# Two ways for the conditional slots of a mixture-of-experts tail: a short one for up to 32 tokens and the full one

## The chip, the cores and the metric

One Trainium2 chip; the program runs on one core. The metric is the device time of one execution in microseconds, here the median of three runs.

## What is computed

An attention layer over 8 batches, 8 heads, 576 positions and 64 dimensions is compressed to 32 memory slots; its output, 4608 rows of 512, goes through a dense ELU network (512 to 2048 to 512), and that through a mixture of 8 experts where each token takes one expert:

```python
logits = x @ w_gate                      # 4608 x 8
expert_idx = np.argmax(logits, axis=1)
gate_w = softmax(logits)[token, expert_idx]
for e in range(8):
    mask = expert_idx == e
    h = np.maximum(x[mask] @ w1[e], 0.0) # 512 -> 1024
    out[mask] = gate_w[mask, None] * (h @ w2[e])
```

Everything is float32. With the inputs that are timed, the reference sends 576, 0, 1152, 576, 1703, 576, 0 and 25 tokens to experts 0 to 7. The first token's expert is 4.

## The kernel before, in words

The attention and the dense network fill the span until about 841 us. They write the rows of `x`, already times the gate, to the DRAM tensor `table`, and the tokens' numbers, sorted by expert, to `itab`. What follows is `phase2`, the expert stage.

Its unit is a **slot**: up to 288 tokens (T) of one expert. Expert 4's first two slots are computed early, while the dense network still runs or just after it (slots -2 and -1). `slots()` then counts on VectorE (DVE) how many slots each expert needs beyond those, and `control()` writes a table `ctl` with a row for each slot j: whether new expert weights must be loaded, and which expert. There are at least 14 more slots (NMIN = 14: numbers 0 to 13) and at most 23 (NS); `tot` says how many there are. For these inputs there are 15, so the slots that run are -2, -1 and 0 to 14. Slots 0 to 13 are written out in line; slots 14 to 22 stand in nested conditionals (`tc.If(end > j)`, L1255) on a register that all engines load from `ends` (L1250). Slot 14 is expert 3's second slot and holds its tokens 289 to 576.

A slot's work, per function:

- `gather(j)` (L715, issued by POOL): three indirect DMAs fetch the tokens' rows into `xr`. `x_store` and `x_load` (L729 and L733, issued by SyncE, SP) pass them through DRAM into `xg`; `x_turn` (L747, DVE) transposes them, and `x_split` (L752 ACT, L753 DVE) writes each value as a rounded part and a rest, `xh` and `xl`.
- `mm1(j, f)` (L1065): 12 TensorE (PE) matmuls into one of two PSUM buffers `ps_h`, then ReLU by ACT (L1068, `hh`) and its rest by DVE (L1069, `hl`), for f = 0 to 7. `mm2(j, f)` (L1080): 12 matmuls into four accumulators.
- `w1_split`, `w2_split` (L1047/1048 and L1053/1054): for the **next** slot, ACT copies 128x512 of the raw weights to the rounded part and DVE subtracts it for the rest; 16 pairs a slot. The conditional slots do them whether or not the next slot exists.
- `evac(j)` (L1088): four DVE transposes from the accumulators into `ot`. `o_store` (L738) writes `ot` to DRAM in four DMAs, all by SP, or two by SP and two by ACT (`TWO`, in the conditional slots). `o_load` (L741, SP) reads them back into `xr` by token, and `scatter` (L1093, POOL) sends them to `out` in three indirect DMAs; places without a token are dropped by the bounds check.
- `load(j, i)` (L1102, L1103, L941): SP loads two registers from `ctl` and issues a weight DMA that moves nothing where its condition is 0.

`columns()` (L1021 to L1029) turns the list of the tokens' numbers by three PE transposes into `idx` and `idw`, the columns from which gather and scatter take their places.

The order of all instructions is written out by hand; each engine takes its own in that order. SP and POOL are first-in, first-out: a DMA that waits holds up all behind it. In `slot(14)` of before, `gather(15)`, `x_store` and `x_load` come first, then the products with two weight splits behind each pair, `load(16, 0)`, `load(16, 1)`, and the store and scatter of slot 14, although slot 15 does not exist. Where a conditional is not taken, each engine instead runs a short block of accounting (rows with L1255 or L1260): it waits for its own work and DMAs that are under way, and raises the semaphores by what the skipped code would have. L1260 is the last conditional (`again`), which is not taken either.

## Time and profile before

| | |
|---|---|
| median of 3 runs | 1319.31 us (1316.88 to 1322.4) |
| profiled execution | 1317.07 us |
| its span, first to last instruction | 1315.4 us |
| busy PE | 1214.9 us (92%) |
| busy DVE | 817.2 us (62%) |
| busy ACT | 674.7 us (51%) |
| busy POOL | 471.4 us (36%) |
| mean granted TensorE clock | 0.973 |

Times in the rows are counted in us from the span's start. Busy shares are means over stages that differ; the stages that matter here are `phase2` from 841 us on, the last conditional slot (1264 to 1290 us), and the way of its result to `out` after that. L numbers are lines of the kernel before. A `q` behind an engine's name marks its sequencer, which branches, waits and issues DMAs.

### The profile page before, as it was taken

To read this page: it belongs to the slowest core of one execution; us is meant where nothing else is said; L and a number is where in the kernel's file an instruction comes from. 1 tells how busy PE (TensorE), PEld (TensorE's weight loads), DVE (VectorE), ACT (ScalarE), POOL (GpSimd) and SP (SyncE) were. 2 spreads that over 40 slices of the span, in tenths; PEclk is the share of its full clock that TensorE was granted. 3 is DMA by queue.
4 is the path that set the end of the run, shared out by engine and by line. 5 is a ranking of instruction groups with operands and counts; after the bars stand their busy time and mean duration, and the time that the engine had idled before them with its cause. 6 is when DMAs were issued, how large, how long until landed. Compare 5 with 4: busy or idle time off the path is not lost.

```text
span 1315.4 us, 26563 instructions
## 1 busy us (share of the span) xinstructions
PE 1214.9 (92%) x10137; PEld 1127.5 (86%) x10137; DVE 817.2 (62%) x1835; ACT 674.7 (51%) x1542; POOL 471.4 (36%) x502
## 2 busy tenths in 40 slices
PE   4497897999999999999999999999999999999992
PEld 2286776889899899898898999999999999999992
DVE  5899764655655656556556545744676767676763
ACT  3686544455555555565555556423444554454441
POOL 2556242443343444434434443411232123222020
PEclk9599998999999999999999999999999999999996
DMA  9776655543544436345432262125587887657633
GB/s 229 201 207 202 186 106 107 131 115 53 137 104 79 131 92 99 102 92 100 133 61 55 70 197 55 37 65 144 154 224 204 261 258 211 197 125 211 178 99 104
DMA packets 116795, 181.38 MB, mean 138 GB/s; under 512 B 11113, under 2 KB 82281, under 8 KB 113072
## 3 DMA queue, kind: packets, MB, share of 16 engines
q1 hardware_dynamic: 107680, 159.15, 47.4%
q0 software_dynamic: 8368, 20.11, 5.4%
q8 instruction: 83, 1.36, 0.5%
q14 instruction: 56, 0.46, 0.2%
q10 hardware_dynamic: 608, 0.30, 0.1%
HBM read 181.78 MB, written 44.47 MB: 172 GB/s over the span
## 4 chain that ended last, share of the span: by engine, by line
PE 71%; DMA 8%; DVE 6%; ACT 6%; issue 4%; POOL 3%; SPq 1%; DVEq 0%; POOLq 0%; ACTq 0%
PE ps_acc L551 23%; PE ps_h L1065 15%; PE ps_h L520 13%; PE ps_acc L1080 13%; PE ps_M L482 2%; DMA kv<-in_v_dram 2%; PE ps_kv L380 1%; DVE e L529 1%; DMA table<-yr 1%; PE ps_s L424 1%; DMA big<-in_q_dram 1%; ACT e L528 1%; DMA xd<-xr 1%; POOL sT L439 1%; ACT e L527 1%
## 5 line engine op out<-in xcount | busy, mean ns | idle before, releaser
L537 POOL TENSOR_TENSOR gl<-e,gh 128x288 fp32r<-128x288 f32 x237 | 195.9, 827 | 389.7 <-ACT gh L536 328.2
L520 PE MATMUL ps_h<-ath,wt 128*128 128x288 f32 x1024 | 261.7, 311 | 9.7 <-DVE e L529 8.4
L529 DVE SCALAR_TENSOR_TENSOR e<-e,ps_h 128x288 f32<-128x288 f32 x256 | 114.9, 449 | 214.5 <-ACT e L528 187.9
L520 PEld LDWEIGHTS ps_h<-ath,wt 128*128 128x128 f32 x1024 | 181.2, 191 | 54.1 <-issue 29.0
L536 ACT CAST gh<-e 128x288 fp32r<-128x288 f32 x256 | 110.3, 432 | 195.2 <-DVE e L529 193.4
L551 PE MATMUL ps_acc<-gh,wt 128*128 128x288 f32 x1024 | 178.3, 296 | 2.6 <-ACT gh L536 2.5
L551 PE MATMUL ps_acc<-gl,wt 128*128 128x288 f32 x1024 | 178.2, 296 | 1.7 <-DVE gl L537 1.7
L551 PE MATMUL ps_acc<-gh,wl 128*128 128x288 f32 x1024 | 178.4, 296 | 0.0
L1065 PE MATMUL ps_h<-xh,wt 128*128 128x288 f32 x1088 | 173.9, 299 | 3.1 <-ACT xh L752 1.6
L1068 ACT ACTIVATE hh<-ps_h 128x288 fp32r<-128x288 f32 x136 | 56.0, 412 | 232.2 <-PE ps_h L1065 214.8
L1065 PEld LDWEIGHTS ps_h<-xh,wt 128*128 128x128 f32 x1088 | 153.2, 188 | 9.6 <-ACT xh L752 5.7
L551 PEld LDWEIGHTS ps_acc<-gh,wt 128*128 128x128 f32 x1024 | 150.4, 189 | 3.8 <-ACT gh L536 3.7
L520 PE MATMUL ps_h<-atl,wt 128*128 128x288 f32 x512 | 152.8, 298 | 0.5 <-POOL atl L470 0.5
L551 PEld LDWEIGHTS ps_acc<-gl,wt 128*128 128x128 f32 x1024 | 150.5, 189 | 2.3 <-DVE gl L537 2.3
L551 PEld LDWEIGHTS ps_acc<-gh,wl 128*128 128x128 f32 x1024 | 151.4, 189 | 0.0
L1069 DVE SCALAR_TENSOR_TENSOR hl<-ps_h,hh 128x288 fp32r<-128x288 f32 x136 | 62.0, 456 | 131.8 <-ACT hh L1068 120.9
L1093 POOL DMA_INDIRECT out_dram<-xr,idw x45 | 47.0, 1043 | 251.0 <-DMA xr<-od 225.9
L527 ACT ACTIVATE e<-ps_h 128x288 f32<-128x288 f32 x256 | 104.6, 409 | 52.0 <-PE ps_h L520 41.8
L528 ACT ACTIVATE e<-e 128x288 f32<-128x288 f32 x256 | 113.8, 445 | 8.1
L520 PEld LDWEIGHTS ps_h<-atl,wt 128*128 128x128 f32 x512 | 98.0, 191 | 0.7 <-POOL atl L470 0.7
L1080 PE MATMUL ps_acc<-hh,wl 128*128 128x288 f32 x640 | 97.9, 294 | 0.0
L1065 PE MATMUL ps_h<-xl,wt 128*128 128x288 f32 x544 | 95.4, 297 | 1.3 <-DVE xl L753 1.3
(194 smaller groups left out, 1948.3 us busy)
## 6 DMA issues: line engine op xcount, KB each, us to landing
raw<-in_moe_w_dram SPq DMA_DIRECT2D x34, 2048.0 KB
win<-win_s SPq DMA_DIRECT2D x28, 1024.0 KB
xd<-xr SPq DMA_DIRECT2D x18, 576.0 KB
xg<-xd SPq DMA_DIRECT2D x72, 144.0 KB
xr<-od SPq DMA_DIRECT2D x17, 576.0 KB
od<-ot SPq DMA_DIRECT2D x66, 144.0 KB
kv<-in_k_dram SPq DMA_DIRECT2D x16, 576.0 KB
kv<-in_v_dram SPq DMA_DIRECT2D x16, 576.0 KB
```

What stands on the lines that cost most here:

```text
L520: nc.tensor.matmul(ps, x[:, u, fo:fo + P], y[:, u], start=(n == 0), stop=(n == 3 * NQ - 1))
L527: nc.scalar.activation(out=e, in_=ps, func=AF.Relu, scale=-1.0)
L528: nc.scalar.activation(out=e, in_=e, func=AF.Exp, scale=-1.0)
L529: nc.vector.scalar_tensor_tensor(out=e, in0=e, scalar=-1.0, in1=ps, op0=ALU.add, op1=ALU.max)
L536: nc.scalar.copy(out=gh, in_=e)
L537: eng.tensor_tensor(out=gl, in0=e, in1=gh.bitcast(F32), op=ALU.subtract)
L551: nc.tensor.matmul(acc[c], x[:, f, P * c:P * c + P], y, start=(first and n == 0), stop=(final and n == 2),)
L1065: nc.tensor.matmul(ps, w1_at(p, y, c, f), x[:, c], start=(n == 0), stop=(n == 3 * NC - 1))
L1068: nc.scalar.activation(out=h, in_=ps, func=AF.Relu)
L1069: V.scalar_tensor_tensor(out=l, in0=ps, scalar=0.0, in1=h.bitcast(F32), op0=ALU.max, op1=ALU.subtract)
L1080: nc.tensor.matmul(acc[c], w2t[p][:, y, f, P * c:P * c + P], x, start=(f + n == 0), stop=(f == NF2 - 1 and n == 2),)
L1093: d = nc.gpsimd.indirect_dma_start(out=out, out_offset=IndirectOffsetOnAxis(ap=at(n), axis=0), in_=xp["r"][:, n], in_offset=None, bounds_c ...
```

## The change

`slot` now does slots 0 to 13 alone, and it loads no weights and fetches no rows for a slot past the 14th. `control()` computes a third column of `ctl`: 2 where a slot holds at most 32 tokens (FEW), else 1; `columns()` makes a fourth transpose and a copy `idf`, the first 32 tokens' numbers. The registers `end`, `again` and this column of slot 14 (`first`) are loaded on all engines ahead of slot 13 and not behind it. A conditional slot then has two bodies under conditionals of their own. `many(j)` is the full slot: it first fetches slot j + 1 (loads, gather, store and load) under a conditional `end > j + 1`, does the products, and makes the 16 weight splits for the next slot in f = 3 to 6, four a step, ahead of `evac`; the transposes and splits of `x` for the next slot stand behind the scatter. `some(j)` multiplies 32 tokens' columns in plain float32, unsplit, straight from the raw weights, and writes them with one scatter.

```diff
--- before.py
+++ after.py
@@ -968,6 +968,7 @@
     V = nc.vector
     NMIN = NT // T - NE
     HN = NF2 // 2
+    FEW = 32
     ONE, TWO = [nc.sync], [nc.sync, nc.scalar]
     w2t = [wl.rearrange("p (y f) n -> p y f n", y=2), None]
 
@@ -981,7 +982,8 @@
     row, sb, rowi = tl(1, "row"), tl(E, "sb"), tl(1, "rowi", I32)
     its = const.tile([NS, T], I32, name="its")
     idx, idw = (const.tile([PR, NG * NS], I32, name=n) for n in ("idx", "idw"))
-    sj, ej, later, ctl, ends = tl(1, "sj"), tl(1, "ej"), tl(1, "later"), tl(2, "ctl", I32), tl(2, "ends", I32)
+    idf = const.tile([FEW, NS], I32, name="idf")
+    sj, ej, later, ctl, ends = tl(1, "sj"), tl(1, "ej"), tl(1, "later"), tl(3, "ctl", I32), tl(2, "ends", I32)
 
     def pick(o, w, x):
         V.tensor_tensor(out=tmp, in0=x, in1=w, op=ALU.mult)
@@ -1013,6 +1015,11 @@
         V.tensor_scalar(out=later, in0=pcol, scalar1=0.0, scalar2=None, op0=ALU.is_gt)
         V.scalar_tensor_tensor(out=ctl[:, 0:1], in0=sj, scalar=pcol, in1=later, op0=ALU.is_equal, op1=ALU.mult)
         V.tensor_copy(out=ctl[:, 1:2], in_=ej)
+        pick(sj, ind, ne)
+        V.tensor_tensor(out=row, in0=row, in1=jm, op=ALU.add)
+        V.scalar_tensor_tensor(out=row, in0=ej, scalar=-float(NR0), in1=row, op0=ALU.mult, op1=ALU.add)
+        V.scalar_tensor_tensor(out=sj, in0=row, scalar=-float(T), in1=sj, op0=ALU.mult, op1=ALU.add)
+        V.tensor_scalar(out=ctl[:, 2:3], in0=sj, scalar1=float(FEW), scalar2=1.0, op0=ALU.is_le, op1=ALU.add)
         V.tensor_copy(out=ends[:, 0:1], in_=tot)
         V.tensor_copy(out=ends[:, 1:2], in_=few)
 
@@ -1024,6 +1031,8 @@
             nc.tensor.transpose(
                 ps[0:PR, NS * n:NS * n + NS], itf.rearrange("j (p n) -> j n p", n=NG)[:, n], ident[0:NS, 0:NS],
             )
+        nc.tensor.transpose(ps[0:FEW, NS * NG:NS * NG + NS], itf[:, 0:FEW], ident[0:NS, 0:NS])
+        V.tensor_copy(out=idf, in_=ps[0:FEW, NS * NG:NS * NG + NS])
         ps = ps[0:PR, 0:NG * NS]
         V.tensor_scalar(out=idx, in0=ps, scalar1=float(NT - 1), scalar2=None, op0=ALU.min)
         V.tensor_copy(out=idw, in_=ps)
@@ -1095,33 +1104,35 @@
                 bounds_check=NT - 1, oob_is_err=False,
             )
             if not alone:
-                tc.declare_no_dep(d.ins, group="rows", reason="a token's row is its own")
-                tc.add_to_no_dep_group("rows", d.ins)
+                rows_out(d)
 
     def load(j, i):
         c, = (nc.values_load(ctl[j:j + 1, 0:1], engines=[SP], min_val=0, max_val=1),)
         ev = nc.values_load(ctl[j:j + 1, 1:2], engines=[SP], min_val=0, max_val=E - 1)
         load_raw(nc, raw[i], (w1, w2)[i], ev, c)
 
-    def slot(j, head, follow):
-        nxt = j + 1 < NS
-        p = (j + 1) % 2
-        if not head and j > 0:
+    def rows_out(d):
+        tc.declare_no_dep(d.ins, group="rows", reason="a token's row is its own")
+        tc.add_to_no_dep_group("rows", d.ins)
+
+    def splits(j, some):
+        for n in some:
+            w1_split(j % 2, n) if n < NF2 else w2_split(j % 2, n - NF2)
+
+    def x_splits(j, some=range(NC)):
+        for c in some:
+            x_split(j, c)
+
+    def slot(j):
+        follow = j + 1 < NMIN
+        if j > 0:
             o_store(ONE)
         if j < NMIN - 1:
             gather(j + 2)
         if 0 < j < NMIN - 1:
             x_store()
-        if not head and j > 0:
+        if j > 0:
             scatter(of(idw, j - 1))
-        if j >= NMIN and nxt:
-            gather(j + 1)
-            x_store()
-            x_load()
-        turn = 3 if j < NMIN else NF2 - 1
-        if head:
-            mm1(j, 0)
-            mm1(j, 1)
         for f in range(NF2):
             if f + 2 < NF2:
                 mm1(j, f + 2)
@@ -1131,30 +1142,84 @@
             if f == NF2 - 1:
                 evac(j)
                 if not follow:
-                    o_store(TWO if j >= NMIN else ONE)
+                    o_store(ONE)
                     scatter(of(idw, j))
-            if nxt:
-                for n in range(2):
-                    if f < HN:
-                        w1_split(p, 2 * f + n)
-                    else:
-                        w2_split(p, 2 * (f - HN) + n)
-                if f == turn:
-                    x_turn(j + 1)
-                    if j >= NMIN:
-                        for c in range(NC):
-                            x_split(j + 1, c)
-                if j < NMIN and f in (4, 5):
-                    for c in range(2):
-                        x_split(j + 1, 2 * (f - 4) + c)
-            if j + 2 < NS and f == HN - 1:
+            splits(j + 1, range(2 * f, 2 * f + 2))
+            if f == 3:
+                x_turn(j + 1)
+            if f in (4, 5):
+                x_splits(j + 1, range(2 * f - 8, 2 * f - 6))
+            if follow and f == HN - 1:
                 load(j + 2, 0)
                 if j == 0:
                     x_store()
-            if j < NMIN - 1 and f == NF2 - 2:
+            if follow and f == NF2 - 2:
                 x_load()
-            if j + 2 < NS and f == NF2 - 1:
+            if follow and f == NF2 - 1:
                 load(j + 2, 1)
+
+    def fetch(j):
+        load(j, 0)
+        load(j, 1)
+        gather(j)
+        x_store()
+        x_load()
+
+    def many(j):
+        nxt = j + 1 < NS
+        if nxt:
+            with tc.If(end > j + 1):
+                fetch(j + 1)
+        mm1(j, 0)
+        mm1(j, 1)
+        for f in range(NF2):
+            if f + 2 < NF2:
+                mm1(j, f + 2)
+            mm2(j, f)
+            if f == NF2 - 1:
+                evac(j)
+                o_store(TWO)
+                scatter(of(idw, j))
+            if nxt and f >= 3 and f < NF2 - 1:
+                splits(j + 1, range(4 * f - 12, 4 * f - 8))
+        if nxt:
+            x_turn(j + 1)
+            x_splits(j + 1)
+
+    def some(j):
+        o = ps_tile(ps_acc, "acc0")[0:FEW]
+        hs = {}
+
+        def close(f):
+            nc.tensor.matmul(
+                o, hs.pop(f), raw[1][:, DM * f:DM * f + DM], start=(f == 0), stop=(f == NF2 - 1)
+            )
+
+        for f in range(NF2):
+            ps = ps_tile(ps_h, "h")[:, 0:FEW]
+            for c in range(NC):
+                n = 2 * HN * P * c + P * f
+                nc.tensor.matmul(
+                    ps, raw[0][:, n:n + P], xp["g"][:, 0, FEW * c:FEW * c + FEW], start=(c == 0), stop=(c == NC - 1)
+                )
+            hs[f] = pool.tile([P, FEW], F32, tag="gh", name="hs", bufs=3)
+            nc.scalar.activation(out=hs[f], in_=ps, func=AF.Relu)
+            if f > 0:
+                close(f - 1)
+        close(NF2 - 1)
+        if j + 1 < NS:
+            with tc.If(end > j + 1):
+                fetch(j + 1)
+                splits(j + 1, range(2 * NF2))
+                x_turn(j + 1)
+                x_splits(j + 1)
+        r = xp["r"][0:FEW, 0]
+        nc.scalar.copy(out=r[:, 0:DM // 2], in_=o[:, 0:DM // 2])
+        V.tensor_copy(out=r[:, DM // 2:], in_=o[:, DM // 2:])
+        rows_out(nc.gpsimd.indirect_dma_start(
+            out=out, out_offset=IndirectOffsetOnAxis(ap=idf[:, j:j + 1], axis=0), in_=r, in_offset=None,
+            bounds_check=NT - 1, oob_is_err=False,
+        ))
 
     b, g = a["b"], a["g"]
     y_logit, y_logit2, y_rank, y_scatter, y_turn, y_gate, y_times, y_store = (
@@ -1244,19 +1309,29 @@
     w2t[1] = a["p1"].enter_context(tc.tile_pool(name="p2", bufs=1, reuse_waits="tile")).tile(
         [P, 2, NF2, DM], F32R, name="w2o"
     )
-    for j in range(NMIN):
-        slot(j, False, j + 1 < NMIN)
+    for j in range(NMIN - 1):
+        slot(j)
     end, again = (
         nc.values_load(ends[0:1, i:i + 1], engines=ALL, min_val=0, max_val=(NS, 1)[i]) for i in range(2)
     )
 
-    def rest(j):
+    def kind(j):
+        return nc.values_load(ctl[j:j + 1, 2:3], engines=ALL, min_val=1, max_val=2)
+
+    first = kind(NMIN)
+    slot(NMIN - 1)
+
+    def rest(j, k):
         if j < NS:
             with tc.If(end > j):
-                slot(j, True, False)
-                rest(j + 1)
-
-    rest(NMIN)
+                k = kind(j) if k is None else k
+                with tc.If(k < 2):
+                    many(j)
+                with tc.If(k > 1):
+                    some(j)
+                rest(j + 1, None)
+
+    rest(NMIN, first)
     with tc.If(again):
         ev = nc.values_load(e0i[0:1, 0:1], engines=[SP], min_val=0, max_val=E - 1)
         early_rows(nc, ev, itab, early_w, NE, NG)
```

## Rows read from the trace of the kernel before

**Rows 1.** Stages: us, busy PE, PEld, DVE, ACT, POOL, clock, DMA share, GB/s.
```profile
925.00:1264.00 339.00, 337.75 (x2496) 332.77 (x2495) 236.49 (x469) 168.44 (x366) 84.56 (x80) 1.00 0.70 199
1264.00:1290.00 26.00, 26.00 (x197) 25.82 (x195) 15.48 (x30) 10.58 (x23) 5.99 (x6) 1.00 0.44 118
1290.00:1303.00 13.00, 0.06 (x1) 0.00 (x0) 5.57 (x14) 2.65 (x6) 0.00 (x0) 0.61 0.56 137
```

**Rows 2.** DMA queues, 1303 to 1310: packets, MB, share of 16 engines.
```profile
q0 software_dynamic: 192, 0.59, 28.7%
```

**Rows 3.** DMA queues, 1103 to 1108, scatter of slot 6.
```profile
q0 software_dynamic: 128, 0.04, 3.0%
```

**Rows 4.** Order of time around `control`: start us, us, engine, line, operation; DVE, PE.
```profile
859.45 0.16 DVE L987 TENSOR_TENSOR tmp<-st,ind 128x8 f32<-128x8 f32 x1
860.62 0.45 DVE L1069 SCALAR_TENSOR_TENSOR hl<-ps_h,hh 128x288 fp32r<-128x288 f32 x1
...
862.04 1.23 PE L1065 MATMUL ps_h<-xh,wt 128*128 128x288 f32 x8
```

**Rows 5.** Chain that ended last, 875 to 923: start us, us, what.
```profile
874.93 0.38 PE ps_m L1024 x3
875.33 0.23 DVE idx L1028
875.56 0.15 DVE idw L1029
...
923.01 0.77 PE ps_h L1065 x2
```

**Rows 6.** Order of time in slot 14: PE, then DVE.
```profile
1264.42 1.22 PE L1065 MATMUL ps_h<-xh,wt 128*128 128x288 f32 x8
1277.16 1.23 PE L1065 MATMUL ps_h<-xh,wt 128*128 128x288 f32 x8
...
1279.41 0.46 DVE L1069 SCALAR_TENSOR_TENSOR hl<-ps_h,hh 128x288 fp32r<-128x288 f32 x1 [1.37 <-issue]
1286.37 2.49 DVE L1054 TENSOR_TENSOR w2o<-raw,w2o 128x512 fp32r<-128x512 f32 x4
1289.70 1.58 DVE L1088 STREAM_TRANSPOSE ot<-ps_acc 128x288 f32<-128x288 f32 x4 [0.85 <-PE ps_acc L1080]
```

**Rows 7.** Order of time, o_store and o_load, slots 13 and 14.
```profile
1265.82 1.97 SPq L738 DMA_DIRECT2D od<-ot  x4
1270.31 0.31 SPq L741 DMA_DIRECT2D xr<-od  x1
...
1291.31 0.86 ACTq L738 DMA_DIRECT2D od<-ot  x2
...
1293.04 1.92 SPq L738 DMA_DIRECT2D od<-ot  x2
1298.12 0.31 SPq L741 DMA_DIRECT2D xr<-od  x1
```

**Rows 8.** L1255 on POOL from 1300, L1310: ns min/median/max, first to last us.
```profile
L1255 POOLq EVENT_SEMAPHORE  x4: 17/43/2417, 1305.1 to 1306.9; - x4
L1255 POOLq COMPARE_BRANCH  x2: 38/44/50, 1304.6 to 1310.2; - x2
...
L1310 SPq EVENT_SEMAPHORE  x14: 17/28/28, 1311.7 to 1315.3; - x14
```

**Rows 9.** The same view: branches of PE (L1255) and DVE (L1260).
```profile
L1255 PEldq COMPARE_BRANCH  x3: 86/196/3914, 1263.1 to 1291.7; - x3
...
L1260 DVEq COMPARE_BRANCH  x1: 62/62/62, 1304.0 to 1304.0; - x1
L1260 DVEq EVENT_SEMAPHORE  x1: 21/21/21, 1306.3 to 1306.3; - x1
```

**Rows 10.** Waits of SP, 1260 to 1316: us in total, times, longest.
```profile
SPq L1255 <- SPq L1255: 3.1, 1, 3.1
```


## What the change will do to the time

> **What bounds the kernel now.** I read the stages first, by windows. From 925 us to the end of slot 13, PE is busy for 337.75 of 339 us, and in slot 14's own 26 us without a gap [rows 1]. So whatever delays PE ahead of 925 us arrives at the end undiminished, and nothing that runs beside PE in slots 1 to 13 counts. After 1290 us PE is idle: 25 us are left in which slot 14's result goes to DRAM, back, and out. That tail is a chain of single steps, and each one there is worth its full price.
>
> Next I asked which slots run. The DMA view of the last scatter shows 192 packets and 0.59 MB, which is 288 rows of 2 KB: slot 14 is full [rows 2]. The only slot with few tokens is number 6, whose scatter moved 0.04 MB [rows 3]. It is one of the 14 in line and does not get the short way. So with these inputs `some` is not entered; slot 14 goes through `many`. What is left of the change is its overhead and what `many` reorders. The order of time around `control`, the chain at `columns`, slot 14, its store, and the exit from the conditionals give the prices.
>
> **The change, part by part.**
>
> *`control`: six more small DVE operations.* The nine that are there start at 859.45 us and hand over at 860.62 us to a `hl` [rows 4]: 1.17 us, 0.13 us each. At that rate six cost 0.8 us; as a dependent chain, each as long as the first one's 0.16 us and a little more, up to 1.2 us. I take 1.1. The `hl` of 0.45 us frees the `ps_h` buffer for the product that PE starts at 862.04 us [rows 4]. It would end at 860.62 + 0.45 + 1.1 = 862.17: PE waits **0.2 us** (0 to 0.3). The later `hl`s catch up while ACT is idle.
>
> *`columns`: one transpose and one copy ahead of `idx`.* Three transposes take 0.38 us on the chain, so the fourth 0.13; a copy like `idw` takes 0.15 [rows 5]. Together **0.3 us** (0.25 to 0.4), before POOL can gather slot 0. From there the chain runs through gather, store, load, scatter and the next gather to a PE that waits for slot 1's `x` until 923.01 us [rows 5]. Nothing on it has slack, and PE is full afterwards [rows 1].
>
> *Slots 0 to 13.* Their order is the old one. The registers loaded before slot 13 instead of behind it lie ahead of work in the queues; PE's branch into slot 14 is at 1263.1 us, the first product at 1264.42 [rows 6, 9], so PE's sequencer ran 1.3 us ahead even after its register loads. If that cover were gone, three loads would cost PE about 1 us. On SP they stand before the store of slot 12; behind it wait only o_load and scatter of slot 12, which nobody needs for the next 20 us. The two weight DMAs that slot 13 no longer issues moved nothing. I count **0**.
>
> *The head of slot 14.* Two branches that fall through and one that is taken, over a fetch block that is empty for PE, ACT and DVE. PE's short branches take 0.09 to 0.2 us [rows 9], inside the 1.3 us of lead (which grows by the register loads that are gone). **0**; if the taken one had to fetch code, PE's long branch of 3.9 us [rows 9] less some 2 us of lead gives 1.9. SP and POOL run an accounting block here that waits for slot 13's store, load and scatter; the next that either has to do is slot 14's store at 1292 us. Hidden.
>
> *Splits crowded into f = 3 to 6.* PE's pair of products takes 3.2 us. Today the products for f = 5 begin at 1277.16 and their `hl` at 1279.41 [rows 6]. Four splits take DVE 2.49 us when they run together [rows 6], and a pitch of 0.60 us when `hl` follows. So I set up DVE's queue from 1279.41: `hl`, four splits to 1282.4; the next `hl` (one pair later, 1282.6) and four to 1285.6; the last `hl` at 1285.8, four to 1288.8; and four more, for f = 6, to 1291.1. `evac` stands behind these, and today it starts at 1289.70, when PE lets it [rows 6]. It moves by **+1.4 us** (0.9 to 1.6), and ends at 1292.7 instead of 1291.3. PE itself waits for none of it: `hl` is ready two products before its use.
>
> *Store and load of slot 14.* Today ACT issues its half at 1291.31, as `evac` ends; SP, which stands behind slot 15's `x_load` and the registers of `load(16)`, only at 1293.04. `o_load` follows at 1298.12, 6.8 us after `evac` [rows 7]. All of that queue is gone. In slot 13, where SP has only the store to do, four issues take 1.97 us and `o_load` follows 4.5 us after the first [rows 7]. With two issues on each of two queues, 1 us less: 3.5 us. So **-3.3 us** (-1.7, if the 5.1 us from SP's first issue to `o_load` stay; -3.5 at best).
>
> *The exit.* Once its last scatter has landed, POOL leaves one accounting block at 1310.2 us, does that of `again`, and lets SP's first closing wait go at 1311.7 [rows 8]: 1.5 us a block. `many` adds one, that of `some` not taken: **+1.5 us**, since both stand in POOL's order behind the wait for the landing. And the long branch out of the nest now comes after that wait. Today it is taken ahead of it, at 1304.6, with the next instruction at 1305.1 [rows 8]: 0.5 us at least. SP waits 3.1 us in its own [rows 10], DVE 2.3 us in its second one, 1304.0 to 1306.3 [rows 9]. Today POOL has only six DMAs to skip in a slot, where DVE and SP skip thirty and more instructions; after the change POOL has ten with three accounting blocks in between, so I take DVE's, **+2.3 us** (0.5 to 3.1).
>
> The Trainium skill, "Advanced Engine Details and Errata", section Control Flow Timing, gives about 51 ns for a branch and 108 ns for a compare-and-branch; by that the long branch would be 0.1 us and the sum 2.2 us lower. SP's and DVE's rows speak against it. "Runtime: NRT & Kernel Launch" there, section Instruction fetch mechanics, says that a taken branch whose target is not among the two pages held must fetch it first; by that the sum stands, and the rows of SP and DVE agree, that of POOL only if its target was at hand.
>
> **Sum.** 0.2 + 0.3 + 1.4 - 3.3 + 1.5 + 2.3 = +2.4 us. On the profiled execution of 1317.07 us that is 1319.5. The median of the runs is 2.2 us higher, 1319.31, so I predict 1319.31 + 2.4 = **1321.7 us**. Lowest: 0.25 + 0.9 - 3.5 + 1.5 + 0.5 = -0.4; highest: 0.7 + 1.6 - 1.7 + 1.5 + 3.1 + 1.9 (PE's head) = +7.1.
>
> **The rivals.**
>
> *POOL's long branch stays cheap.* Its target is at hand, as today, and costs 0.5 us: the sum is +0.6, 1319.9 us. For it: POOL's row. Against it: a stream for POOL that is about three times as long a slot.
>
> *Every taken branch fetches.* The code of a slot now spreads over two bodies and their accounting, and even the short jumps over a block leave what the engine holds. The place is POOL's exit: four taken branches after the landing (out of one block, over the nest, to and out of `again`) at DVE's 2.3 to SP's 3.1 us, say 2.6, instead of one; and PE's head with 1.9. Sum: 0.5 + 1.4 - 3.3 + 1.5 + 10.4 + 1.9 = +12.4 us, 1331.7: slower. It decides from about 1.1 us a branch. Against it: today's POOL takes two branches behind its landing, and the whole block between is 1.5 us [rows 8]; PE's middle branch is 0.2 [rows 9].
>
> *The short way is taken in slot 14.* Then 25 us of products shrink to forty short ones; at three small ones in 0.38 us [rows 5], 5 us, some 20 us less: 1299 us, faster. It needs a slot 14 with at most 32 tokens; 0.59 MB say 288 [rows 2].
>
> *The short way does nothing at all here and the rest cancels*: 1319.3, within the forecast's range.
>
> **How the numbers follow.** A measurement of this kernel can tell about 0.5% (6.6 us) from no change. The forecast 0.50; POOL's branch cheap 0.30; cancelling 0.07; every branch fetching 0.09; the short way taken 0.03; the last 0.01 is for what I did not see. All but the second and the third rival lie within 0.5%. That makes faster 0.04, same 0.87, slower 0.09. For the range I take the forecast's ends and the cheap branch, and below it the 2.4 us by which the lowest run shown lies under the median: 1316.5 to 1326.5.
>
> **What would show it.** Right: the last scatter at 1303 us still moves 0.59 MB; no L715 and L733 rows after 1270; `evac` of slot 14 starts 1.4 us behind the last product's release, with splits in front of it; SP's store follows within 0.1 us, `o_load` some 3.5 us after `evac`; POOL has two accounting blocks of L1255's kind after the landing, with a gap of 2 us or more ahead of the second. Wrong: a PE gap at slot 14's head, a gap at each of POOL's branches, or slots whose products are 128x32. The step I trust least is the price of POOL's long branch; next the 3.5 us from `evac` to `o_load`.

## The result, and the profile after

The changed kernel took 1326.16 us (median of 9 runs, 1322.17 to 1331.11), the kernel before, beside it on the same chip, 1318.69 us (9 runs, 1315.98 to 1322.4). The ratio is 1.0054, with a 95% interval from 1.0036 to 1.0073. That is 7.1 us more where I had forecast 2.4; the time lies inside the range, close to its upper end. (The two medians themselves differ by 7.5 us.) Two later comparisons of the same two programs gave smaller ratios (below). The profiled execution took 1323.09 us, its span 1321.3.

All that the change could do to the end happens behind slot 14's products. To compare executions that start their expert stage at different times, I count from slot 14's first `hh`. This row of ACT's order of time (start us, us, engine, line, operation) gives it for the kernel before:

```profile
1266.27 0.41 ACT L1068 ACTIVATE hh<-ps_h 128x288 fp32r<-128x288 f32 x1 [2.20 <-PE ps_h L1065]
```

And the same order of time after the change, all engines but PE, from that `hh` to the last scatter; it answers to [rows 6, 7]:

```profile
1270.13 0.41 ACT L1077 ACTIVATE hh<-ps_h 128x288 fp32r<-128x288 f32 x1 [1.94 <-PE ps_h L1074]
...
1291.44 3.70 DVE L1063 TENSOR_TENSOR w2o<-raw,w2o 128x512 fp32r<-128x512 f32 x6
...
1295.05 1.57 DVE L1097 STREAM_TRANSPOSE ot<-ps_acc 128x288 f32<-128x288 f32 x4
...
1296.65 0.81 SPq L738 DMA_DIRECT2D od<-ot  x2
1296.65 0.88 ACTq L738 DMA_DIRECT2D od<-ot  x2
...
1302.57 0.32 SPq L741 DMA_DIRECT2D xr<-od  x1
1308.60 0.91 POOL L1102 DMA_INDIRECT out_dram<-xr,idw  x1 [25.79 <-SPq L1330]
...
1311.05 0.92 POOL L1102 DMA_INDIRECT out_dram<-xr,idw  x1 [0.30 <-issue]
```

`evac` (L1097) stands right behind six weight splits and starts 24.92 us after slot 14's first `hh`; before, it was 1289.70 - 1266.27 = 23.43, released by PE [rows 6]. SP and ACT now issue their halves of the store in the same moment, 0.03 us after `evac`'s end; before, SP was 1.7 us later than ACT [rows 7]. But `o_load` still follows 5.95 us after `evac`'s end, not 3.5.

Slot 14 is full, as forecast: the last scatter moved as much as in [rows 2]. DMA queues of the kernel after, 1308 to 1316 us (packets, MB, share of 16 engines):

```profile
q0 software_dynamic: 192, 0.59, 25.5%
q14 instruction: 6, 0.05, 2.2%
```

The exit on POOL, three lines of the code (L1330: the short way's conditional, L1326: the nest, L1335: `again`), with instruction, count, ns min/median/max, first to last start; it answers to [rows 8]:

```profile
L1330 POOLq COMPARE_BRANCH  x1: 55/55/55, 1309.8 to 1309.8; - x1
L1330 POOLq INC_SWDGE_SEM  x1: 763/763/763, 1311.6 to 1311.6; - x1
...
L1326 POOLq EVENT_SEMAPHORE  x4: 17/30/43, 1315.3 to 1315.6; - x4
L1326 POOLq COMPARE_BRANCH  x2: 43/44/45, 1312.4 to 1316.5; - x2
L1326 POOLq INC_SWDGE_SEM  x1: 787/787/787, 1315.6 to 1315.6; - x1
...
L1335 POOLq INC_SWDGE_SEM  x1: 760/760/760, 1317.1 to 1317.1; - x1
...
L1385 SPq EVENT_SEMAPHORE  x14: 17/28/28, 1317.8 to 1321.2; - x14
```

The order of the three blocks is the one forecast. What differs is the place of the landing. The block of the short way (L1330) ends at 1312.4, only 0.4 us after the last scatter's issue ended at 1311.97; it waits for earlier DMAs, not for this landing. The long branch over the nest leaves at 1312.4 and POOL's next instruction is at 1315.3: 2.9 us. Before, the wait for the landing is POOL's longest one, 2417 ns from 1306.9 [rows 8], and ends 2.2 us after the last scatter's issue did (1307.14), 0.36 us after the scatter's last packet (1308.93). Here the last packet ends at 1313.42, so by the same 0.36 us POOL could have gone on at some 1313.8 (an estimate), while the branch is still under way: 1.5 us of it stick out, and no block stands wholly behind the landing that did not before. Some 0.4 us come back in what follows, most of it in POOL's longest closing DRAIN (the first of these lines is from the kernel before):

```profile
L1310 POOLq DRAIN  x3: 51/107/2763, 1311.7 to 1315.1; - x3
L1385 POOLq DRAIN  x3: 46/106/2518, 1317.9 to 1321.0; - x3
```

The terms, from three profiled executions of the changed kernel (the result's, e2 and e11 below) and two of the kernel before (that of the rows and e1), in us from slot 14's first `hh`:

| | before | after | moved | forecast |
|---|---|---|---|---|
| end of `evac` | 25.01, 25.01 | 26.49, 26.49, 26.48 | +1.48 | +1.4 |
| `evac`'s end to `o_load` | 6.84, 6.40 | 5.95, 5.90, 5.94 | -0.69 | -3.3 |
| `o_load` to the end of the last scatter's issue | 9.02, 8.91 | 9.39, 8.96, 9.40 | +0.29 | 0 |
| from there to the span's end | 8.22, 8.20 | 9.32, 9.44, 9.39 | +1.17 | +3.8 |
| span's end | 49.09, 48.52 | 51.15, 50.79, 51.21 | +2.25 | +1.9 |

The third row moved without a forecast, but it lies anywhere from 8.65 to 9.56 us in the fourteen profiled executions of all kernels here; what moves it is not shown.

The two profiled spans differ by 5.9 us, though. The rest lies ahead of the expert stage. ACT's `hh` of all 17 slots, from slot -2's first on, ns min/median/max, first to last start, in the kernel before, in another execution of the same kernel (e1), and in the changed one:

```profile
L1068 ACT ACTIVATE hh<-ps_h x136: 405/412/415, 842.8 to 1285.3; 128x288 fp32r<-128x288 f32 x136
```

```profile
L1068 ACT ACTIVATE hh<-ps_h x136: 399/410/415, 849.2 to 1292.3; 128x288 fp32r<-128x288 f32 x136
```

```profile
L1077 ACT ACTIVATE hh<-ps_h x136: 404/412/419, 847.7 to 1289.3; 128x288 fp32r<-128x288 f32 x136
```

The stage's first `hh` (slot -2's) comes 4.9 us later in the changed kernel, but no instruction ahead of it was touched, and the kernel before itself reaches it at 842.8 in one execution and at 849.2 in another.

### The profile page after: what moved, and what is told of

It reads as the page before. It is cut to its first block, busy times and chain, and to the rows that moved or that the text cites. A ratio compares the mean times of both kernels' runs of the same rounds, so it can differ in the third digit from the quotient of the medians.

```text
span 1321.3 us, 26578 instructions
## 1 busy us (share of the span) xinstructions
PE 1217.0 (92%) x10138; PEld 1129.2 (85%) x10138; DVE 818.2 (62%) x1842; ACT 675.0 (51%) x1542; POOL 464.6 (35%) x499
```

## The experiments

Two theories for the 7.1 us. **Theory**: the change costs the tail some 2.2 us and the control a few tenths, and the rest is the variation of the stages ahead. **Rival**: it has a systematic cost ahead of slot -2, where no instruction was touched, by the places of tiles in memory (the new tile `idf` and the wider `ctl` move later tiles by 96 bytes) or by the larger program. For the tail: which part costs what, and why the store did not get faster by 3.3 us.

**e1, e2, e11: the kernel before against itself, and the changed kernel twice more.** No edit.

> The kernel before, once more, as a null comparison and a second profile. In the profiles at hand the changed kernel is 5.9 us longer in its span, and 4.9 us of it are there when the expert stage's first product (L1065) starts: 842.8 us's hh before, 847.7 after, ahead of every instruction that the change touches. Chance theory (the early part differs from one execution to the next): ratio 1.000, and the first hh here falls several us away from 842.8. Placement theory (96 bytes by which the new tiles move others in SBUF) and code theory (a longer program): ratio 1.000 and the first hh within 1.5 us of 842.8.

> The changed kernel, once more. All theories: ratio 1.003 to 1.007. Chance theory: the first hh of the expert stage lands anywhere from 841 to 849 us; if its excess was chance, the ratio falls to what the exit costs, 2 us or 1.0015. Placement and code theory: first hh again at 846 to 849 us, ratio 1.005 again. The stretch from slot 14's first product to the end of the span is 51.2 us again (49.1 before) by every theory.

> The changed kernel once more, beside the other two. Parts theory: 50.8 to 51.2 us from slot 14's first hh to the end, 2.1 us more than before, ratio 1.0016; the first comparison's 1.0054 was made by the early part, which no instruction of the change touches, and should not come again. Rival (the change costs 5 us or more that the profiles do not show): ratio 1.004 or more again.

The kernel before against itself: 0.9984 (0.9963 to 1.0005), and its first `hh` 6.4 us away from 842.8, as chance asked and neither rival did. The changed kernel: 1.0005 (0.9981 to 1.0028) and 1.0038 (1.0013 to 1.0062), after 1.0054 the first time. The 1.0005 lies below what every theory had asked for; its interval holds the 1.0015 to which chance alone could bring it. The interval of e11 holds both its theory's 1.0016 and its rival's 1.004, so e11 decides nothing. The intervals of the first and the second do not overlap, so the interval of one comparison is narrower than what there is between comparisons. The medians say which side moved: the changed kernel had 1326.16, 1326.03 and 1326.97 us, the kernel before, beside it, 1318.69, 1322.96 and 1322.93. By medians the change costs 7.5, 3.1 and 4.0 us. The second and the third comparison ran on two different chips, so the chip may be part of what differs between comparisons. Tails agree far better: 50.8 to 51.2 us in all three executions (table above).

**e3: the shift in memory alone.**

```diff
+    idf = const.tile([32, NS], I32, name="idf")
+    nc.vector.memset(idf, 0)
-    sj, ej, later, ctl, ends = tl(1, "sj"), tl(1, "ej"), tl(1, "later"), tl(2, "ctl", I32), tl(2, "ends", I32)
+    sj, ej, later, ctl, ends = tl(1, "sj"), tl(1, "ej"), tl(1, "later"), tl(3, "ctl", I32), tl(2, "ends", I32)
```

> The kernel before with the new tile idf and the third column of ctl allocated but not used (one memset): its tiles behind them in SBUF stand 96 bytes on, as in the changed kernel. Placement theory: first hh 4 to 5 us later, ratio 1.004 (1318.7 to 1323.5 us). Chance and code theory: ratio 1.000.

1.0015 (0.9985 to 1.0044): not told from 1, nor from the 1.004 that the placement theory asked for. In its profiled execution the stage's first `hh` came at 857.7 us, the latest of all. That was the slowest of its 12 runs, 1336.88 us where their median is 1326.52, and one execution doesn't say that the shift did it.

```profile
L1070 ACT ACTIVATE hh<-ps_h x136: 403/412/415, 857.7 to 1304.8; 128x288 fp32r<-128x288 f32 x136
```

**e4: a larger program.** Before, with many more instructions inside the last conditional, which is not taken.

```diff
     with tc.If(again):
         ...
+        for _ in range(30):
+            for n in range(NG):
+                early_gather(-NE, n, rows)
+            x_store()
+            x_load()
+            for n in range(NF2):
+                w1_split(0, n)
+                w2_split(0, n)
         ...
+            x_turn(j)
+            for f in range(NF2):
+                mm1(j, f)
+                mm2(j, f)
+            evac(j)
```

> The kernel before with more code in the last conditional, which is not taken: about as many more instructions on ACT and DVE as the change adds (506 and 514), 385 on PE, 242 on SP, 120 on POOL, and no tile moved. Code theory: first hh 4 to 5 us later, ratio 1.004. Chance and placement theory: ratio 1.000, apart from longer jumps at the end (under 3 us).

1.0014 (0.9994 to 1.0034), the stage's first `hh` at 847.5, tail 50.02 us. The interval ends below the 1.004 that the code theory asked for: code that is skipped costs nothing that shows in the whole time. The tail is 0.5 us longer than the longest other one of this order (e3, 49.52), most of it between `evac` and `o_load` (7.35 us).

**e5: the splits two a step again.** Changed kernel; `evac` gets its old place.

```diff
-            if nxt and f >= 3 and f < NF2 - 1:
-                splits(j + 1, range(4 * f - 12, 4 * f - 8))
+            if nxt:
+                splits(j + 1, range(2 * f, 2 * f + 2))
```

> The changed kernel with the weight splits for the next slot spread again, two in each of the eight steps, instead of four in f = 3 to 6. Counted from slot 14's first hh, two profiles of the changed kernel have evac at 24.9 us, its end at 26.5, o_load at 32.4, the last scatter's end at 41.3 to 41.8 and the end at 50.8 to 51.2; two of the kernel before 23.4, 25.0, 31.4 to 31.9, 40.3 to 40.9 and 48.5 to 49.1. Crowding theory (DVE's queue holds evac back, and all behind it moves along): evac at 23.4, o_load at 30.9, end at 49.5. Rival (o_load waits for something that evac does not set, such as a code fetch at a fixed time): evac at 23.4, o_load still near 32, end near 50.8.

One execution: 1322.93 us. `evac` ends at 25.10 us, 1.39 earlier, which shows the price of the crowding. But the tail ends at 48.25, 2.8 us earlier than the mean of the changed kernel and 1.2 earlier than the crowding theory asked for: `o_load` follows `evac` after 4.65 us and not 5.95. Order of time, SP and ACT:

```profile
1298.08 1.90 SPq L738 DMA_DIRECT2D od<-ot  x2
1298.08 1.88 ACTq L738 DMA_DIRECT2D od<-ot  x2
...
1302.70 0.32 SPq L741 DMA_DIRECT2D xr<-od  x1
```

The DMA queues suggest why the same store's reader is issued 1.3 us earlier. The store is 1216 packets, half on q1 and half on q10. In the first 4 us after its issue, the changed kernel (1296.65 to 1300.65):

```profile
q10 hardware_dynamic: 578, 0.28, 36.0%
q1 hardware_dynamic: 602, 0.29, 35.3%
q8 instruction: 1, 0.02, 1.4%
```

and e5 (1298.08 to 1302.08):

```profile
q10 hardware_dynamic: 608, 0.30, 38.9%
q1 hardware_dynamic: 581, 0.29, 38.6%
```

The profile calls q8 and q14 instruction queues: their packets are code being fetched. In the changed kernel one 16 KB packet of q8 began in these 4 us, a second and three of q14 in the 1.5 us after them (1300.65 to 1302.10), while the last packets of the store were still to go:

```profile
q14 instruction: 3, 0.02, 11.0%
q8 instruction: 1, 0.02, 6.8%
```

Both q8 packets (1299.7 and 1300.8) began while PE stood in its branch over `again`:

```profile
L1335 PEldq COMPARE_BRANCH  x1: 5702/5702/5702, 1298.2 to 1298.2; - x1
```

In e5 none begins in its 4 us. One began just ahead of them, at 1298.02, and ran beside the first half microsecond of the store's data, to 1299.35; the next began at 1302.14, as the store's last packets ended. A window from 1297.90 to 1302.08 counts the first:

```profile
q8 instruction: 1, 0.02, 2.0%
```

**e7: PE kept in straight code.** To take the fetch away and nothing else from the store, PE got 96 more products behind slot 14's last, whose result nobody reads; so its branches come 13 us later.

```diff
                 scatter(of(idw, j))
+                for _ in range(8):
+                    ps = ps_tile(ps_h, "h")[:, 0:T]
+                    for n in range(12):
+                        nc.tensor.matmul(ps, w1_at(j % 2, 0, 0, 0), xp[j][0][:, 0], start=(n == 0), stop=(n == 11))
```

> The changed kernel with 96 products of 128x288 that nothing reads behind slot 14's last: PE stays in straight code for some 13 us more, so that its branches, and the 16 KB code fetches behind them, come after slot 14's store has landed. In the changed kernel 15 of 16 parts of the store's last DMA are in 3.9 us after evac's end, the last one after 5.9. Fetch theory (a code packet of 0.9 to 1.6 us sits in one of the 16 DMA engines ahead of the store's part): o_load 3.5 to 4.3 us after evac's end, in place of 5.9. Rival (the store on ACT's queue is slow in itself): 5.9 us again. The end may still be late by what PE adds.

One execution: 1324.4 us. `evac` ends at 26.48 us as in the changed kernel, and `o_load` follows after 4.83 us: not the 5.9 of the rival, but 0.5 us over the 3.5 to 4.3 asked for. Queues, 1297.99 to 1301.99; no q8:

```profile
q10 hardware_dynamic: 603, 0.29, 37.0%
q1 hardware_dynamic: 608, 0.30, 35.8%
```

So PE's fetches cost the store 1.1 us. The landings, read from the traces, show where. Each of the store's four DMAs lands in 16 parts, and `o_load` follows the last part of all by 0.1 to 0.2 us in every run. Of the second DMA on q1, 15 parts were in 4.17 us after `evac` in the changed kernel, the last at 5.55 (not the expectation's 3.9 and 5.9); in e7 all 16 were in at 4.06. On q10 the last part came at 5.75 and at 4.62. One or two parts wait, and with them the reader.

The time came back at the exit, 11.1 us from the last scatter to the end instead of 9.4: POOL's long branch took 4.1 us instead of 2.9, from 1312.6 to 1316.7, while PE's late branch (5.1 us from 1312.3) was under way. That the two fetches slow each other fits but is not shown.

```profile
L1330 POOLq EVENT_SEMAPHORE  x4: 17/30/43, 1316.7 to 1316.9; - x4
L1330 POOLq COMPARE_BRANCH  x2: 43/44/45, 1312.6 to 1317.9; - x2
...
L1339 PEldq COMPARE_BRANCH  x1: 5080/5080/5080, 1312.3 to 1312.3; - x1
```

**e6: no short way.** Changed kernel without `some` and the two conditionals around the bodies.

```diff
-                k = kind(j) if k is None else k
-                with tc.If(k < 2):
-                    many(j)
-                with tc.If(k > 1):
-                    some(j)
+                many(j)
```

> The changed kernel without some and without the two inner conditionals: every conditional slot goes through many, the rest of the change stays. From the last scatter's end to the end of the span the changed kernel takes 9.3 to 9.4 us, the one before 8.2. Exit theory (the accounting block of the way not taken, and the long branch behind it): 8.2 us, and only two blocks of POOL; end at 49.8 us from slot 14's first hh. Rival (the nest's length alone makes it): 9.3 us. The way from evac's end to o_load stays at 5.9 us unless code fetches set it: with fewer branches of PE behind its last product it may fall below 5.5.

One execution: 1321.05 us, tail 47.95 us. The exit is 7.79 us, 1.6 less than the changed kernel's, since the wait for the landing is again the first thing that holds POOL, behind the long branch. That branch itself is short again, too: 0.5 us to POOL's next instruction (1309.2 to 1309.7), as in the kernel before, and not 2.9. POOL, L1326, answering to the rows after above:

```profile
L1326 POOLq EVENT_SEMAPHORE  x4: 17/43/2188, 1309.7 to 1311.2; - x4
L1326 POOLq COMPARE_BRANCH  x2: 38/42/45, 1309.2 to 1314.2; - x2
L1326 POOLq INC_SWDGE_SEM  x1: 764/764/764, 1313.5 to 1313.5; - x1
```

The branch leaves at 1309.2, before the scatters' issue is done, and the 2188 ns wait ends at 1313.4. `o_load` is 0.9 us closer to `evac`, and the last scatter 0.6 us closer to `o_load`. The end comes 1.9 us earlier than the exit theory asked for.

**e8, e9, e10: one conditional with an alternative in place of two.** In e8 `some` stands in the `Else` of `many`'s conditional; e9 moves fetch and splits for the next slot behind the scatter, into the conditional that asks whether there is one; e10 is e8 with the splits of e5.

```diff
-                with tc.If(k < 2):
+                with tc.If(k < 2) as cmp:
                     many(j)
-                with tc.If(k > 1):
+                with cmp.Else():
                     some(j)
```

> The changed kernel with the short way as the other branch of one conditional (if and else) in place of two conditionals. Exit theory: no accounting block of its own for the way not taken, the long branch comes directly behind the last scatter's issue and its fetch beside the landing: 8.0 to 8.4 us from the last scatter's end to the end, in place of 9.3 to 9.4, and end at 49.8 to 50.1 us from slot 14's first hh. Rival (the bigger code): 9.3 us again. The ratio of the whole time can't show 1 us: 1.000 to 1.004.

> The changed kernel with if and else for the two ways, and with all work for the next slot (fetch, splits, transposes) in the conditional behind the scatter: with these inputs slot 14 does none of it. Parts theory (the stretch from slot 14's first hh to the end is the sum of DVE's queue, the store with its code fetches, and the exit; 50.8 to 51.2 us in the changed kernel, 48.3 with even splits, 49.4 with else): evac at 23.4, o_load 4.5 to 6 us after evac's end, 8.1 us from the last scatter's end to the end; 47 to 48 us in all, ahead of the kernel before (48.5 to 49.1). Rival (one conditional more behind the scatter gives it back): exit over 9 us, 48.5 or more. Whole time: 1 to 2 us under the kernel before, which the ratio can hardly show: 0.997 to 1.001.

> The changed kernel with if and else, and with the weight splits spread two a step. Parts theory: the two savings add: evac at 23.5, exit 8.1 us, 46.7 to 47.7 us from slot 14's first hh to the end. Rival (they share a cause, the code fetches): 48 us or more. Ratio 0.997 to 1.001.

| | `evac` ends | to `o_load` | exit | tail ends | ratio to before |
|---|---|---|---|---|---|
| e8 | 26.46 | 5.96 | 8.11 | 49.43 | 1.0019 (0.9995 to 1.0044) |
| e9 | 25.08 | 6.90 | 8.09 | 49.63 | 1.0015 (0.9993 to 1.0037) |
| e10 | 25.08 | 6.81 | 8.39 | 49.75 | 1.0017 (0.9996 to 1.0038) |

The `Else` saves the block: the exit is 1.3 us shorter than with two conditionals, as its theory said. POOL's long branch is still 2.8 us, 1309.5 to 1312.3, but it runs beside the landing, for which POOL then waits another 1050 ns:

```profile
L1326 POOLq EVENT_SEMAPHORE  x5: 17/43/1050, 1312.3 to 1312.6; - x5
L1326 POOLq COMPARE_BRANCH  x2: 43/49/55, 1309.5 to 1314.5; - x2
```

Against e8, e9 and e10 free `evac`, 1.4 us, and lose all of it again: 0.9 us between `evac` and `o_load`, 0.6 between `o_load` and the last scatter. Their theories had asked for 47 to 48 and 46.7 to 47.7 us in all; both missed. For e10 the rival's 48 us or more came. For e9 it came too, but not for its reason, the exit. In e10 two 16 KB packets fall into the first 4 us (1296.92 to 1300.92), with 4.9% of the engines' time:

```profile
q10 hardware_dynamic: 593, 0.29, 36.2%
q1 hardware_dynamic: 605, 0.29, 35.4%
q8 instruction: 2, 0.03, 4.9%
```

So what e5 gained at this place it owed not to the even splits as such: with the `Else` they meet the fetches.

**e12: what is left when the undone parts are put together.** The changed kernel without the short way, its column of `ctl` and `idf`, and with even splits; of the change there stays that a conditional slot fetches the next one only where there is one.

```diff
-                k = kind(j) if k is None else k
-                with tc.If(k < 2):
-                    many(j)
-                with tc.If(k > 1):
-                    some(j)
+                many(j)
...
-            if nxt and f >= 3 and f < NF2 - 1:
-                splits(j + 1, range(4 * f - 12, 4 * f - 8))
+            if nxt:
+                splits(j + 1, range(2 * f, 2 * f + 2))
```

> The changed kernel without its short way: no body for few tokens, no third column of the control table, no list idf, the weight splits at two a step again. What stays of the change is that a conditional slot fetches the next one only if there is one. Counted from the first hh of slot 14, where the kernel before ends at 48.5 to 49.1 us and the changed one at 50.8 to 51.2. If the two undone parts add (even splits alone: 48.25, no short way alone: 47.95): o_load 29.8 us, 0.9 us less at each of two places, last scatter 39.2 us, end 46.4 to 47.0 us, 2 us ahead of the kernel before; the columns' transposes come 32.03 us after slot 0's first hh, as before. If the DMA landings or the code fetches just meet other work (rival): o_load at 31 us or later and the end at 48 us or later. In the whole time 2 us are 0.15 percent: ratio to the kernel before 0.998 to 1.000, which hardly tells from 1; a ratio above 1.002 would say that something outside the tail, which varies between executions, carries the difference.

0.9989 (0.9961 to 1.0017); medians 1318.72 against 1322.0 us. The tail ends at 47.39 us, 1.4 us ahead of the kernel before; the undone parts do not simply add. It had to be 46.4 to 47.0 for that, 48 or more for the rival, and lies between, because `o_load` came 5.82 us after `evac`, with two 16 KB packets in the first 4 us (1288.29 to 1292.29) and fewer of the store's own done:

```profile
q1 hardware_dynamic: 581, 0.28, 35.8%
q10 hardware_dynamic: 562, 0.27, 34.3%
q8 instruction: 2, 0.03, 4.6%
```

It is the shortest tail of all, yet 1.4 us are 0.1%, and the whole time does not show that it beats the kernel before. Its profiled span of 1310.7 us owes more to the early stage (its first `hh` of the stage at 840.5 us) than to the tail.

## Why the prediction was right, and where its terms were not

*What bounds, and which way is taken.* Right. The last scatter moved 0.59 MB, the products have slot 14's full shape, and `some` cost only what surrounds it.

*`control`, +0.2 us.* Its own rows fit, an arrival at the end does not show (under *Slots 0 to 13*): the columns' transposes stand 32.2 us after the stage's first `hh` in all nine executions with the longer `control`, 32.0 in the kernel before, e1, e4 and e12. First and last of the six added DVE operations, and the `hl` that follows them, answering to [rows 4]; 865.37 to 866.22 and 0.15 make 1.0 us, where I took 1.1:

```profile
865.37 0.16 DVE L989 TENSOR_TENSOR tmp<-ne,ind 128x8 f32<-128x8 f32 x1
...
866.22 0.15 DVE L1022 TENSOR_SCALAR ctl<-sj 128x1 int32<-128x1 f32 x1
...
866.41 0.45 DVE L1078 SCALAR_TENSOR_TENSOR hl<-ps_h,hh 128x288 fp32r<-128x288 f32 x1
```

*`columns`, +0.3 us.* Too small at POOL; at PE not to be told. Counted from the stage's first `hh`, the first gather starts at 33.82 us and not at 33.00, 0.8 later: 0.2 is `control`'s, 0.1 the fourth transpose and the copy, and 0.5 lies between `idw` and the gather, which no row of mine explains. The operations, all engines:

```profile
880.42 0.17 DVE L1035 CAST idf<-ps_m 32x23 int32<-32x23 f32 x1 [0.89 <-PE ps_m L1034]
880.52 0.21 DVE L1037 TENSOR_SCALAR idx<-ps_m 96x69 int32<-96x69 f32 x1
880.65 0.21 DVE L1038 CAST idw<-ps_m 96x69 int32<-96x69 f32 x1
...
881.53 0.94 POOL L715 DMA_INDIRECT xr<-table,idx  x1 [13.94 <-DVE idw L1038]
```

Where PE would meet it, at slot 1's first `hh`, two executions of the kernel before differ by 0.6 us (81.05 and 80.45), and three of the changed one lie at 80.38 to 80.78.

*Slots 0 to 13, and the head of slot 14, 0.* As far as can be told, right: from the stage's to slot 14's first `hh` it is 422.4, 424.6 and 423.5 us after, 423.4 and 424.0 before; and PE's last product ends 23.88 us after slot 14's first `hh`, against 23.79. But the 0.5 us of `control` and `columns` should have arrived in the first of these stretches undiminished, and its means are 423.5 after and 423.7 before. With 2 us between executions it neither shows the 0.5 us nor excludes them.

*Crowded splits, +1.4 us.* Right: +1.48, and e5, which undoes them, gives 1.39 back. I set up DVE's queue by hand from two pitches of rows 6; that is worth the trouble.

*Store and load, -3.3 us.* The step that failed, by 2.6 us. I took slot 13's 4.5 us from the first issue to `o_load` [rows 7] for what an unhindered store takes, and a further 1 us off because two queues issue. The issues did not set it. What sets it is the landing of all parts. `o_load` came 4.65 to 5.0 us after `evac` where none (e7) or one (e5, e6) of the 16 KB code packets ran beside the store's data, 5.8 to 6.9 us where two did (the changed kernel, e8, e9, e10, e12), early in the data (e12) or late. The first number is the term I should have had, some 4.7 us, a gain of 1.9; the fetches, a further 1.2 us, I did not look for, though the kernel before has them too. Against e5 the crowding has a second price, since it moved the store into PE's fetch; but e9, e10 and e12, whose `evac` is as early as e5's, met the fetches as well. What was measured, -0.69, lies outside the bounds that I gave this term, -1.7 to -3.5.

*The exit, +1.5 + 2.3 = +3.8 us.* The mechanism was there, the order was wrong, and the sum came to 1.17, below the least that I allowed (1.5 + 0.5). POOL's long branch cost 2.7 to 2.9 us in the three executions, more than I took. The Trainium skill, "Runtime: NRT & Kernel Launch", section Instruction fetch mechanics, has a taken branch whose target is not held wait for its page to be fetched; POOL's 2.9 us agree with that, as the rows of SP and DVE did: two of the q14 packets shown above begin in them, at 1313.5 and 1313.7. The 0.5 us of the kernel before and of e6 do only if the target was at hand there. But I put the short way's block and the branch behind the wait for the landing, and they ran beside it: that block's last instruction starts at 1311.6, before the issue of the last scatter is over, so it waits for earlier DMAs only. e6 and e8, each with one block fewer and the long branch beside the landing, have exits of 7.8 and 8.1 us: block and place of the branch are worth 1.3 to 1.6 us together.

*The sum.* For the tail +1.9 was forecast and +2.25 measured, but as a sum of two wrong terms with opposite signs: -3.3 should have been -0.7, +3.8 should have been +1.2. That they cancel is luck. The whole time fell inside the range by luck, too: its upper end was made of a fetch at PE's head and a dearer exit, and neither came; the rest of the 7.1 us lies elsewhere (below). A right total proves no term.

*The rivals.* That every taken branch fetches fell: POOL's two others on the way out take 0.2 us or less to the next instruction, as 1316.5 to 1316.6. That POOL's long branch stays cheap fell in the changed kernel: 2.9 us, where the rival has 0.5. Without the short way and its conditionals (e6) it is 0.5 us again, with the short way under an `Else` (e8) 2.8: the short way's code in the nest made it dear. The short way was not entered.

*The whole time.* 7.1 us in the first comparison, 0.7 and 5.0 us in the others (1.0005 and 1.0038 of some 1322 us), or 7.5, 3.1 and 4.0 us by medians. The traces account for 2.25 us at the tail, and for 0.2 to 0.4 at the control if that arrives. Beyond that the spans of the changed kernel and the kernel before differ in the early stage. Its end, the first `hh` of slot -2, lies at 847.6 to 849.6 us in all nine profiled executions with `idf` and the longer `ctl` in use, at 840.5, 842.8, 847.5 and 849.2 in the four with the old places, and at 857.7 in e3. A cost of the shift of some 2 us would fit these numbers, and so would chance; e3's ratio of 1.0015 excludes neither. Whether there is such a part stays open.

## What to carry to other kernels

This conditional was paid for at the exit: count the accounting blocks that each engine passes after the last product, ask of each which DMAs it waits for, and set the branches beside the landing before adding them to it. Code that is never entered counts as well, where a branch has to jump over it (0.5 us without the short way, 2.9 with it). A store whose landing is on the critical path is better issued well before the engines branch, because their code packets held back its parts here (e7): 1.1 us, and up to 2 in e9 and e10, as much as the reordering that was meant to gain it. And where an effect is 0.2%, compare stages counted from a common instruction; the whole time of two comparisons of the same programs here differed by 0.5%.

## What the runs showed of the hardware that was not expected

- Two 16 KB code packets beside the 1216 of a store can hold back the last of them: `o_load` 4.65 to 5.0 us after `evac` with none (e7) or one (e5, e6), 5.8 to 6.9 us with two. That one alone does it is not shown: e6, with one, had 5.0.
- A long branch of POOL took 2.9 us to its next instruction (1312.4 to 1315.3), and 4.1 us where PE branched at the same time (e7); over a nest without the short way it took 0.5 us (before, e6), and short branches took 0.2 us.
- The same kernel reached the same instruction (slot -2's first `hh`) at 842.8 us in one execution and at 849.2 us in another.
